# A new order of steps beside the weight conversions, and own orders for the first two periods, in a fused attention and squared-ReLU kernel

## The chip, the cores and the metric

The kernel runs on one core of one Trainium2 chip. The metric is the device time of one launch in microseconds (us), the median of several runs. The profile is one execution of the program, with every instruction of the engines: PE (matmuls; PEld is its weight load), DVE (vector), ACT (scalar, activations), POOL (GpSimd) and SP, which only issues DMAs.

## The reference

Thresholded attention over 8 batches of 8 heads, 576 positions, head size 64; its output, 4608 tokens of 512, goes through a two-layer network.

```python
def _attn_ref(q, k, v, tau):
    scale = 1.0 / np.sqrt(q.shape[-1])
    scores = scale * np.matmul(q, k.transpose(0, 1, 3, 2))
    thresh = np.max(scores, axis=-1, keepdims=True) - tau
    scores = np.where(scores >= thresh, scores, -1000000000.0)
    scores = scores - np.max(scores, axis=-1, keepdims=True)
    attn = np.exp(scores)
    attn = attn / (np.sum(attn, axis=-1, keepdims=True) + 1e-09)
    return np.matmul(attn, v)

def _moe_ref(x, w_in, w_out):          # x: (4608, 512), w_in: (512, 2048), w_out: (2048, 512)
    h = np.maximum(x @ w_in, 0.0)
    return h * h @ w_out
```

The inputs q, k and v are float32; the two weight matrices come as float64, so each weight is two 32-bit words, a low and a high one.

## The kernel before

The kernel has three stages: attention, from the start to about 512 us; the hidden layer (L825); and the output layer (L960). The two layers use a scheme with fewer block products and many block sums; the change touches only the attention.

Attention works on pairs of heads (32 pairs) in units. A unit is 128 query rows of one pair, and after the four units of each of two pairs comes one unit that holds the last 64 rows of both: 144 units. A *period* p handles the pair of units A = 2p and B = 2p + 1. `period(p)` runs a list of named steps, each of which issues instructions; an engine executes its own instructions in the order in which the list names them, and waits only on semaphores. So the list sets the order on each engine, and a step far down one engine's queue may hold up another engine. There is one period from p = -2 to p = 74; scores start at p = 0, and the values' matmuls of a pair of units follow two periods later.

The steps of a period, with the engine and the line in the profile:

- SA, SB (PE, L434): scores of the units A and B into the banks of the PSUM tile `sc`. SA also writes the last 64 keys of both units, into banks 1 and 4; SB writes banks 2 and 3, SA's main part banks 0 and 5.
- topA0, topA1, topB0, topB1 (DVE, L452): copy a head's 576 scores from PSUM to SBUF, with the (negated) maximum accumulated.
- leastA, leastB (POOL, L459, 128x2): the threshold of both heads of a unit, from the two tops.
- powA0 ... powB1 (ACT, L462): the exponential.
- maskA0 ... maskB1 (DVE, L467): compare the scores with the threshold and multiply by the exponential, with the sum accumulated; both inputs are in SBUF. The masks need the power and the least.
- over (POOL, L474) and inv (DVE, L477): the sum plus 1e-9 and its reciprocal, for the previous period's units.
- U, V, W (PE, L380 and L515): transposes of the weights in three parts, U and V into the two banks of the pool `pt`, which has one buffer, W into banks 2 and 3 of `sc`; eU, eV, eW (ACT, L523) evict them.
- T (PE, L398) transposes queries or keys of a coming pair; eT (ACT, L403 and L411) evicts them, scaled where they are queries, and asks for the next loads of queries or keys on SP's queue. T's places are `spots()`, parts of the banks 1 and 4 of `sc`.
- PV (PE, L532): the values' matmuls into banks 0 and 5; x (ACT in a converting period, DVE in others) copies them out, xm (POOL, L654) multiplies them by the reciprocal, issues the next load of values and the writes of x.
- fetch, c1 to c6: conversion of one weight chunk (128 x 512 float64) to float32. fetch loads the chunk of period p + 2; c1 (ACT, L205) takes the absolute value of the high words; c2 (POOL, L212) scales the low words by 2^-29; c3 (POOL, L219) clamps the high words; one period later c4 (DVE, L227, shift and mask), c5 (DVE, L235, merges the sign, two inputs in SBUF) and c6 (POOL, L245, adds the low words).

Chunks are begun in the periods 2 to 33, so the periods 2 to 34 are *converting* ones and use the list CONVERTING; the others use PLAIN. The touch function orders instructions that share a PSUM bank: an instruction waits for the last one of each other engine that touched the same bank.

The beginning is written out: loads of the first pair, 15 warm-up transposes of PE (`keep_busy`), the turns of the first pair, then the periods; after period 0 come 20 more warm-up transposes (L1012).

Of the kernel before, what the change touches and what calls it, by code (L numbers as in the profile page):

```python
# [10 lines left out]
FP32 = mybir.dt.float32  # L11
# [37 lines left out]
def kernel(  # L49
# [27 lines left out]
    P = 128  # L77
# [7 lines left out]
    BANK = 512  # L85
# [305 lines left out]
    def turn(i, which, spots, other=None):  # L391

        nat, to = loaded.pop((i, which)), places(i)
        of = [nat[:, t, :] for t in range(FULL)] + ([loaded.pop((i, 2))] if which else [])
        for t, x in enumerate(of):
            for r, (spot, at) in enumerate(spots):
                rows = ds(r * HALF, HALF)
                made = nc.tensor.transpose(spot[:, ts(t, HALF)], x[rows, :], ident[rows, rows])  # L398
                touch("turns", made, at, BANK)
        half = FULL * HALF  # L400

        def scaled(to, spot):
            touch("turned", nc.scalar.activation(out=to, in_=spot[0], func=AF.Identity, scale=qscale[:, :]), spot[1], BANK, i)  # L403

        def then():
            part = lambda r, x, n: (spots[r][0][:, ds(x, n)], spots[r][1])
            if which:
                for r, n in ((0, half), (1, half + REST)):
                    spot = part(r, 0, n)
                    copy_by = other if r and other else nc.scalar.copy  # L410
                    touch("turned", copy_by(to[1][:, ds(r * half, n)], spot[0]), spot[1], BANK, i)  # L411
                scaled(to[2], part(0, half, REST))
                ask_ahead(i, 1)
            else:
                for r in range(2):
                    scaled(to[0][:, ds(r * half, half)], part(r, 0, half))
                ask_ahead(i, 0)

        return then
# [68 lines left out]
    for g in range(2, 2 * len(pairs)):  # L488
        two, x = divmod(g - 4, 4)
# [93 lines left out]
    def converts(p):  # L583
        return is_wide and (has_chunk(p) or has_chunk(p - 1))

    def has_chunk(p):
        return p in starts

    def begun(n):
        return starts.get(n)  # L590

    PLAIN = """
# [2 lines left out]
        maskB1  # L595
    """.split()
    CONVERTING = """
        fetch SA U eU T SB topA0 s1 c1 topA1 topB0 c3 V PV leastA over powA0 topB1
        powA1 powB0 c4 eT inv x maskA1 maskA0 W leastB maskB0 c5 eV c2 powB1 c6 eW maskB1 xm
    """.split()  # L600

    def spots():
        return [(sc[:, ds(b * BANK + REST, (FULL + 1) * HALF)], b * BANK) for b in (1, 4)]
# [4 lines left out]
    def period(p):  # L608

        A, B_, a, b = 2 * p, 2 * p + 1, 2 * p - 2, 2 * p - 1  # L610
        m, turns = p - 2, TURNS.get(p, ())
        late, pt = {"W": []}, {}

        def fills(f, m):
            if has(2 * m):
                pt[f] = pt_pool.tile([P, 2, BANK], FP32, tag="pt", name="pt")
                fill(m, f, pt[f])

        def evict(f, m):
            if has(2 * m):  # L620
                filled(m, f, pt[f], 2 * BANK if f == "W" else None)

        def W():
            if has(2 * m + 2):
                pt["W"] = middle()
                fill(m + 1, "W", pt["W"], 2 * BANK)

        def turn_some():
            late["turn"] = [turn(g // 2, g % 2, spots()) for g in turns]

        def PV():
            if has(2 * m):
                values(m)

        def values_out():
            if not has(2 * m):
                return
            late["x"] = x = sb.tile([P, 2, P], FP32, tag="x", bufs=2, name="x")
            for j in range(2):
                from_ = sc[:, ds(5 * j * BANK, P)]  # L640
                if converts(p):
                    made = nc.scalar.copy(x[:, j, :], from_)
                else:
                    made = nc.vector.tensor_tensor(  # L644
                        out=x[:, j, :], in0=from_, in1=wT[m][:, ts(SCALE_AT + j, P)], op=ALU.mult
                    )
                touch("x", made, 5 * j * BANK, P, m)

        def given_out():
            if has(2 * m):  # L650
                x = late.pop("x")
                if converts(p):
                    both = x[:, :, :].rearrange("p j n -> p (j n)")
                    nc.gpsimd.tensor_tensor(out=both, in0=both, in1=wT[m][:, ds(SCALE_AT * P, 2 * P)], op=ALU.mult)  # L654
                wT.pop(m)
                valued(m)
                give_x(m, x)
            ask(False)

        def scored_a():  # L660
            if has(A):
                scores(A, False)
                scores(A, True)
                scores(B_, True)
                softmax(A)

        def scored_b():
            if has(A):
                scores(B_, False)
                softmax(B_)  # L670

        def every(key):
            for then in late.get(key, ()):
                then()

        steps = {
            "U": lambda: fills("U", m), "V": lambda: fills("V", m + 1), "W": W, "T": turn_some,
            "eU": lambda: evict("U", m), "eV": lambda: evict("V", m + 1), "eW": lambda: evict("W", m + 1),
            "eT": lambda: every("turn"),
            "SA": scored_a, "SB": scored_b,  # L680
            "PV": PV, "x": values_out, "xm": given_out,
            "c1": lambda: convert1(begun(p)), "c2": lambda: convert2(begun(p)),
            "c3": lambda: convert3(begun(p)), "c4": lambda: convert4(begun(p - 1)),
            "c5": lambda: convert5(begun(p - 1)), "c6": lambda: convert6(begun(p - 1)),
            "s1": lambda: sums_due(p) and sums_step(), "s2": lambda: sums_due(p) and p < 60 and sums_step(), "fetch": lambda: fetch(begun(p + 2)),
        }
        steps["over"] = lambda: do(a, "over")
        steps["inv"] = lambda: do(a, "inverse")
        for letter, n in (("A", A), ("B", B_)):
            for what, name in (("least", "least"),):  # L690
                steps[what + letter] = lambda n=n, name=name: do(n, name)
            for what, name in (("top", "top"), ("pow", "power"), ("mask", "mask")):
                for j in range(2):
                    steps[f"{what}{letter}{j}"] = lambda n=n, name=name, j=j: do(n, name, j)
        for name in CONVERTING if converts(p) else PLAIN:
            steps[name]()
        for n in (A, B_):
            if has(n) and units[n][1] == FULL:
                for i in units[n][0]:
                    turned.pop(i)  # L700
# [301 lines left out]
    with tc.manual_schedule():  # L1002
        with ExitStack() as stack:
            sc = stack.enter_context(tc.tile_pool(name="sc", bufs=1, space=PSUM)).tile([P, 6 * BANK], FP32, name="sc")
            pt_pool = stack.enter_context(tc.tile_pool(name="pt", bufs=1, space=PSUM))

            def keep_busy(times, to=None):

                if to is None:
                    to = pt_pool.tile([P, 2, BANK], FP32, tag="pt", name="idle")[:, 0, 0:P]  # L1010
                for _ in range(times):
                    nc.tensor.transpose(to, ident[:, :], ident[:, :])  # L1012

            load_q(0)
            load_k(0)
            read_tau()
            first = sb.tile([P, 4, 4], FP32, tag="small", bufs=4, name="small")
            nc.scalar.activation(out=first[:, 0, :], in_=ident[:, 0:4], func=AF.Exp)
            load_v(0)
            keep_busy(15)  # L1020
            pq = pt_pool.tile([P, 2, BANK], FP32, tag="pt", name="pq")
            turn(0, 0, [(pq[:, r, :], None) for r in range(2)])()
            keep_busy(8, sc[:, ds(5 * BANK, P)])
            turn(0, 1, spots(), nc.vector.tensor_copy)()
            for i in range(1, 3):
                load_v(i)
            for p in range(-2, NU // 2 + 3):
                period(p)
                if p == 0:
                    keep_busy(20)  # L1030
                if X_FIRST <= p < X_FIRST + 4:
                    load_x(0, XPARTS[p - X_FIRST :][:1])
                if p == X_FIRST + 4:
                    summing.append(prepare_x(0, lambda op, out, x, y: op(nc.gpsimd, out, x, y)))
            for _ in range(60):
                sums_step()
            ask()
# [186 lines left out]
```

## Time and profile before

| what | value |
|---|---|
| median of 3 runs | 1308.91 us (1307.8 to 1309.66) |
| the profiled execution | 1308.12 us, span 1306.3 us |
| busy over the span | PE 98%, DVE 77%, ACT 65%, POOL 70% |
| masks (L467) | x288, 237.4 us, 860 ns mean |
| tops (L452) | x288, 205.0 us, 747 ns mean |
| low-word scaling c2 (L212) | x32, 65.1 us, 2035 ns mean |
| clamp c3 (L219) | x32, 19.6 us, 613 ns mean |
| c6 (L245) | x32, 1.48 us each |
| least (L459) | x144, 65.3 us, 453 ns mean |
| warm-up after period 0 | x20, 2.40 us from 11.41 us |

A line of the timeline has the start in us, the duration in us, engine, line of the kernel, operation, output and inputs with their sizes, and in brackets the idle time of that engine ahead of it with what ended it. On DVE a row's duration runs on a little into the next row, so lengths are best taken from start to start. The means of a group mix rows beside other work with rows alone.

### The profile page before, as it was taken

What the parts mean: (1) busy time and instruction counts of PE and PEld (TensorE: products, weight loads), DVE (VectorE), ACT (ScalarE), POOL (GpSimd) and SP (SyncE); (2) the same over time, 40 slices, a digit from 0 to 9 for tenths busy, and PEclk for the clock granted to TensorE, in tenths of its full rate; (3) what the DMA queues carried; (4) which work ended last, traced back from release to release, by engine and by line L of the source; (5) the groups of instructions that cost most, each with busy time, mean ns of one, the idle gap of its engine ahead of it and who ended that gap; (6) DMA issues with size and microseconds to landing.
All of it is one profiled execution on the core that took longest, in us unless ns stands there. A gap on an engine that the chain in (4) does not pass through costs nothing.

```text
span 1306.3 us, 47872 instructions
## 1 busy us (share of the span) xinstructions
PE 1284.5 (98%) x19483; PEld 1159.8 (89%) x19483; DVE 1010.8 (77%) x2431; ACT 845.7 (65%) x1498; POOL 916.4 (70%) x1023
## 2 busy tenths in 40 slices
PE   8999999999999999999999999999999999999998
PEld 5777777677777777999999999999999999999998
DVE  5999999999999996877787778777646654665463
ACT  5999999888898985657665766675523432433240
POOL 2777778755555320978897789768777777777775
PEclk9999999999999999999999999999999999999999
DMA  6565666544333313466556665569645234522511
GB/s 153 145 160 140 169 182 188 147 103 104 89 78 79 79 41 80 133 200 218 182 181 194 203 208 164 180 247 393 245 158 162 63 105 158 162 68 96 162 34 33
DMA packets 247035, 192.12 MB, mean 147 GB/s; under 512 B 97184, under 2 KB 195488, under 8 KB 246816
## 3 DMA queue, kind: packets, MB, share of 16 engines
q1 hardware_dynamic: 245504, 188.66, 48.5%
q8 instruction: 153, 2.51, 0.8%
q14 instruction: 66, 0.54, 0.2%
q10 hardware_dynamic: 1312, 0.41, 0.1%
HBM read 116.65 MB, written 72.35 MB: 145 GB/s over the span
## 4 chain that ended last, share of the span: by engine, by line
PE 87%; ACT 5%; DMA 3%; DVE 3%; issue 1%; POOL 1%; SPq 0%; ACTq 0%; DVEq 0%; POOLq 0%
PE po L960 29%; PE ph L825 28%; PE sc L532 11%; PE sc L434 10%; PE pt L380 5%; DVE arena L452 3%; ACT arena L462 2%; PE sc L515 2%; DMA wall<-w 2%; PE sc L398 2%; ACT arena L523 1%; PE sc L380 1%; DMA g<-arena 1%; ACT arena L403 0%; ACT c L771 0%
## 5 line engine op out<-in xcount | busy, mean ns | idle before, releaser
L125 POOL TENSOR_TENSOR arena<-arena 128x512 f32<-128x512 f32 (+1 forms) x314 | 378.1, 1223 | 129.1 <-DVE arena L125 115.1
L960 PE MATMUL po<-wall,arena 128*128 128x128 f32 x3528 | 394.7, 275 | 1.4 <-ACT arena L737 1.4
L960 PEld LDWEIGHTS po<-wall,arena 128*128 128x128 f32 x3528 | 394.3, 192 | 1.8 <-ACT arena L737 1.8
L825 PE MATMUL ph<-arena,wall 128*128 128x128 f32 x3528 | 394.2, 275 | 0.7 <-DVE arena L644 0.7
L825 PEld LDWEIGHTS ph<-arena,wall 128*128 128x128 f32 x3528 | 394.0, 192 | 0.8 <-issue 0.8
L125 DVE TENSOR_TENSOR arena<-ph,arena 128x512 f32<-128x512 f32 x378 | 256.3, 688 | 86.3 <-PE ph L825 63.2
L122 POOL TENSOR_TENSOR arena<-arena 128x128 f32<-128x128 f32 (+2 forms) x314 | 255.4, 814 | 53.8 <-DMA arena<-w 37.6
L125 DVE TENSOR_TENSOR arena<-po,arena 128x128 f32<-128x128 f32 x378 | 108.4, 290 | 168.6 <-PE po L960 164.5
L467 DVE SCALAR_TENSOR_TENSOR arena<-arena 128x576 f32<-128x576 f32 x288 | 237.4, 860 | 1.3 <-POOL arena L459 0.8
L452 DVE TENSOR_SCALAR_CACHE_REDUCE arena<-sc 128x576 f32<-128x576 f32 x288 | 205.0, 747 | 14.6 <-ACT arena L523 4.8
L462 ACT ACTIVATE arena<-arena 128x576 f32<-128x576 f32 x288 | 208.1, 773 | 11.8 <-DVE arena L452 8.5
L771 ACT COPY c<-arena 128x512 f32<-128x512 f32 (+1 forms) x303 | 173.5, 579 | 49.6 <-DVE arena L122 41.7
L532 PEld LDWEIGHTS sc<-arena 64*64 64x64 f32 x5760 | 159.2, 133 | 36.7 <-DVE arena L452 20.2
L532 PE MATMUL sc<-arena 64*64 64x128 f32 (+1 forms) x5760 | 180.8, 262 | 2.7 <-DVE arena L452 1.3
L434 PE MATMUL sc<-arena 64*64 64x64 f32 (+1 forms) x2304 | 176.9, 414 | 6.2 <-ACT arena L403 4.2
L122 DVE TENSOR_TENSOR arena<-arena,c 128x512 f32<-128x512 f32 (+1 forms) x267 | 174.9, 663 | 5.5 <-ACT c L771 4.0
L523 ACT COPY arena<-pt 128x1024 f32<-128x1024 f32 x144 | 146.4, 1017 | 30.5 <-PE pt L380 29.4
L737 ACT COPY arena<-po 128x128 f32<-128x128 f32 x63 | 16.6, 264 | 186.7 <-PE po L960 184.0
L380 PEld LDWEIGHTS pt<-ident,arena 64*128 64x128 f32 x2304 | 83.4, 139 | 39.4 <-ACT arena L523 30.1
L737 ACT COPY arena<-ph 128x512 f32<-128x512 f32 x63 | 36.6, 581 | 123.1 <-PE ph L825 122.5
L434 PEld LDWEIGHTS sc<-arena 64*64 64x64 f32 x2304 | 74.3, 134 | 45.1 <-ACT arena L403 15.1
L380 PE MATMUL pt<-ident,arena 64*128 64x64 f32 x2304 | 102.2, 228 | 2.3 <-ACT arena L523 2.3
(50 smaller groups left out, 922.2 us busy)
## 6 DMA issues: line engine op xcount, KB each, us to landing
g<-arena SPq DMA_DIRECT2D x144, 256.0 KB, 2.6
arena<-g SPq DMA_DIRECT2D x144, 256.0 KB, 4.6
w<-arena SPq DMA_DIRECT2D x60, 256.0 KB, 2.4
wall<-w SPq DMA_DIRECT2D x49, 256.0 KB, 5.2
arena<-w SPq DMA_DIRECT2D x44, 256.0 KB, 3.3
arena<-in_v_dram SPq DMA_DIRECT2D x32, 288.0 KB, 4.0
out_dram<-arena SPq DMA_DIRECT2D x70, 128.0 KB, 2.2
arena<-in_q_dram SPq DMA_DIRECT2D x64, 128.0 KB, 4.0
```

The costliest lines, as they stand in the source:

```text
L122: e.tensor_tensor(out=out, in0=x, in1=y, op=ALU.subtract)
L125: e.tensor_tensor(out=out, in0=x, in1=y, op=ALU.add)
L380: made = nc.tensor.transpose(pt[:, r, ts(slot, HALF)], of[rows, :], ident[rows, rows])
L434: made = nc.tensor.matmul(sc[at, ds(to, count)], lhs, kT[rows, ds(at_k, count)], start=True, stop=True)
L452: made = nc.vector.tensor_scalar(out=s[:, j, :], in0=sc[:, ds(at, S)], scalar1=1.0, scalar2=None, op0=ALU.mult, op1=ALU.min, accum_out=nmx ...
L462: nc.scalar.activation(out=w[:, :, j, :], in_=of(j), func=AF.Exp, bias=nmx[:, j : j + 1], scale=-1.0)
L467: nc.vector.scalar_tensor_tensor(out=w[:, :, j, :], in0=of(j), scalar=thr[:, j : j + 1], in1=w[:, :, j, :], op0=ALU.is_le, op1=ALU.mult, a ...
L523: touch("weights", nc.scalar.copy(joined(to), whole(pt, 0, count)), at, 2 * BANK, m)
L532: made = nc.tensor.matmul(sc[ds(u * D, D), ds(5 * j * BANK + row, count)], loaded_v[i][rows, (c - (u != j)) % CH, :], wT[m][rows, ds(weigh ...
L771: nc.scalar.copy(c, y)
L825: nc.tensor.matmul(to[:, j, :], W_IN[m, k][:, ts(j, P)], of[k][:, m - 1, :], start=(not more and j == 0), stop=True, skip_group_check=True,)
L960: nc.tensor.matmul(to, g[:, j, :], w[:, j, :], start=(not more and j == 0), stop=(j == 3), skip_group_check=True)
```

## The change

Three things change. The list of the converting periods is replaced by another one. The periods 0 and 1 get lists of their own, `BEGIN_WITH`, in place of PLAIN. In periods below 2 the turned queries and keys go to a tile of the pool `pt`, instead of the spots in the banks 1 and 4 of `sc`, where scores are written too. Around the first turn, the loads of the second pair's queries and keys are asked for ahead of the first values' load, and the 20 warm-up transposes after period 0 are left out. No computation is added or removed.

```diff
     CONVERTING = """
-        fetch SA U eU T SB topA0 s1 c1 topA1 topB0 c3 V PV leastA over powA0 topB1
-        powA1 powB0 c4 eT inv x maskA1 maskA0 W leastB maskB0 c5 eV c2 powB1 c6 eW maskB1 xm
+        s1 fetch SA T U c1 topA1 topA0 leastA eU SB over topB0 PV c2 powA1 powA0 maskA1
+        powB0 topB1 c4 eT inv x V powB1 leastB maskA0 maskB0 c3 c5 eV W maskB1 c6 xm eW
     """.split()
+
+    BEGIN_WITH = {
+        0: """
+            SA SB fetch topA0 T topA1 leastA topB0 topB1 leastB powA0 powA1 eT powB0 powB1
+            maskA0 maskA1 maskB0 maskB1
+        """.split(),
+        1: """
+            SA SB T eT fetch over topA0 topA1 leastA inv V topB0 topB1 leastB powA0 powA1 eV W
+            powB0 eW maskA0 maskA1 powB1 maskB0 maskB1
+        """.split(),
+    }
...
         def turn_some():
-            late["turn"] = [turn(g // 2, g % 2, spots()) for g in turns]
+            free = None
+            if turns and p < 2:
+                pq = pt_pool.tile([P, 2, BANK], FP32, tag="pt", name="pq")
+                free = [(pq[:, r, :], None) for r in range(2)]
+            late["turn"] = [turn(g // 2, g % 2, free or spots()) for g in turns]
...
-        for name in CONVERTING if converts(p) else PLAIN:
+        for name in BEGIN_WITH.get(p) or (CONVERTING if converts(p) else PLAIN):
             steps[name]()
...
             nc.scalar.activation(out=first[:, 0, :], in_=ident[:, 0:4], func=AF.Exp)
+            ask_ahead(0, 0)
+            ask_ahead(0, 1)
             load_v(0)
...
             for p in range(-2, NU // 2 + 3):
                 period(p)
-                if p == 0:
-                    keep_busy(20)
```

The order list of PLAIN, which the periods 0 and 1 used, is `SA c3 T topA0 over U eU s1 SB topA1 powA1 leastA topB0 powB0 c1 s2 PV c4 V fetch inv powA0 c5 topB1 powB1 eT maskA1 x xm W eV maskA0 leastB c2 c6 eW maskB0 maskB1`.

## The prediction

> **What bounds the kernel now.** I read the windows first, to see which engine is full in the stretch that the change touches.
>
> ```profile
> 160.00:180.00 20.00, 19.70 (x464) 14.47 (x462) 20.00 (x55) 19.06 (x34) 16.94 (x21) 1.00 0.66 178
> 300.00:320.00 20.00, 19.75 (x546) 14.88 (x540) 19.54 (x60) 17.77 (x28) 11.42 (x15) 1.00 0.49 118
> ```
>
> Columns: PE, PEld, DVE, ACT and POOL busy, clock, DMA share, GB/s. In the converting stretch (first row) DVE is busy 20.00 of 20 us; in the plain one PE is the fullest. So in the 33 converting periods every nanosecond of DVE counts. The period is the distance between two reciprocals (L477): 163.48 to 170.56, 7.08 us; nearly all of them are 7.05 to 7.10, 7.07 in the middle.
>
> Next, the timeline of DVE over one such period, and of POOL beside it.
>
> ```profile
> 163.57 0.78 DVE L467 SCALAR_TENSOR_TENSOR arena<-arena 128x576 f32<-128x576 f32 x1
> ...
> 164.28 1.22 DVE L467 SCALAR_TENSOR_TENSOR arena<-arena 128x576 f32<-128x576 f32 x1
> ...
> 165.43 0.81 DVE L467 SCALAR_TENSOR_TENSOR arena<-arena 128x576 f32<-128x576 f32 x1
> ...
> 166.17 0.68 DVE L235 SCALAR_TENSOR_TENSOR arena<-arena 128x512 int32<-128x512 int32 x1
> 166.78 0.81 DVE L467 SCALAR_TENSOR_TENSOR arena<-arena 128x576 f32<-128x576 f32 x1
> ...
> 167.51 0.75 DVE L452 TENSOR_SCALAR_CACHE_REDUCE arena<-sc 128x576 f32<-128x576 f32 x1
> ```
>
> ```profile
> 163.34 0.38 POOL L459 TENSOR_SCALAR arena<-arena,tau_p 128x2 f32<-128x2 f32 x1
> 163.79 2.04 POOL L212 TENSOR_SCALAR arena<-arena 128x512 int32<-128x512 uint32 x1
> 167.00 1.48 POOL L245 TENSOR_TENSOR arena<-arena 128x512 int32<-128x512 int32 x1 [1.17 <-DVE arena L235]
> 168.44 0.72 POOL L654 TENSOR_TENSOR arena<-arena 128x256 f32<-128x256 f32 x1
> 169.14 0.62 POOL L219 TENSOR_SCALAR arena<-arena 128x512 f32<-128x512 f32 x1
> 169.74 0.30 POOL L459 TENSOR_SCALAR arena<-arena,tau_p 128x2 f32<-128x2 f32 x1
> 170.09 0.23 POOL L474 TENSOR_SCALAR arena<-arena 128x4 f32<-128x4 f32 x1
> ```
>
> From start to start the masks (L467) take 0.71, 1.15, 0.74 and 0.73. The second is long by 0.41 in every converting period: POOL's low-word scaling c2 (L212) began 0.22 into the first mask, so its reading falls to the moment when the second should start. The third mask is not longer, though c2 runs 0.40 into it. The tops (L452, which read PSUM) take 0.68 each beside c6 (L245), xm (L654) and c3 (L219): no cost. So a POOL operation costs DVE time beside an operation that reads two SBUF tiles, and none beside a top. Without the 0.41, DVE's period would be 7.08 - 0.41 = 6.67. ACT's own operations, start to start from 161.37 to 168.30, are about 6.83 (three powers 1.99, turn 0.83, x 0.32, fourth power 0.67, evictions 0.91 + 0.63 + 0.91, c1 0.60): the next floor.
>
> Two more places show how the engines meet. A 128x2 least (L459) that starts inside a mask, and c4 (L227) that starts inside c3:
>
> ```profile
> 13.29 0.81 DVE L467 SCALAR_TENSOR_TENSOR arena<-arena 128x576 f32<-128x576 f32 x1
> 13.47 0.80 POOL L459 TENSOR_SCALAR arena<-arena,tau_p 128x2 f32<-128x2 f32 x1 [1.05 <-DVE arena L452]
> ...
> 233.57 0.61 POOL L219 TENSOR_SCALAR arena<-arena 128x512 f32<-128x512 f32 x1 [0.73 <-ACT arena L205]
> ...
> 233.90 0.56 DVE L227 TENSOR_SCALAR arena<-arena 128x512 int32<-128x512 int32 x1
> ```
>
> The least takes 0.80 instead of 0.30: it ends 0.24 after the mask (14.03). c4 takes 0.56 instead of 0.42: POOL was there first.
>
> **The new converting period.** Nothing is added; the lists decide. DVE's order becomes topA1, topA0, topB0, maskA1, topB1, c4, inverse, maskA0, maskB0, c5, maskB1. POOL's becomes leastA, over, c2, leastB, c3, c6, xm. Put down with the durations above, from the start of topA1:
>
> - DVE without waits: topA0 0.68, topB0 1.36, maskA1 2.03, topB1 2.77, c4 3.45, inverse 3.79, maskA0 3.88, maskB0 4.59, c5 5.33, maskB1 5.94, end 6.67.
> - POOL: c6 starts 0.22 into the last mask, as now, and goes 0.93 past its end (1.44 to xm); xm 0.70 to 1.63; leastA 0.35 to 1.98 (its other input, topA0, is there at 1.5); over 0.33 to 2.31; c2 from 2.31 to 4.34.
>
> c2 thus starts 0.28 into maskA1, nearly as now, but its reading (done 0.88 after its start: 0.49 to the second mask and its 0.41 of delay) falls beside topB1, which costs nothing. So the 0.41 is gone. Three things take its place.
>
> First, leastB stands behind c2 on POOL. It is dispatched at 4.34, inside maskA0 (3.88 to 4.59), and by the 13.47 row ends 0.24 after that mask: 4.83. maskB0 needs it and is next on DVE; with 0.07 for the hand-over (POOL's gap between operations) it starts at 4.90 instead of 4.59: 0.31. Queued behind it are c5 and maskB1, and the next period's tops. Bounds: 0, if c2 is over by 3.6, to 0.31.
>
> Second, c3 moves from beside the tops, where it was free, to behind leastB, at 4.9. From there to 6.67 DVE runs only operations with two SBUF inputs, so c3 reads at one of their borders. It is a one-input 128x512 read as c2 is: 0.41. Bounds: 0, if it slips into a gap, to 0.47 (how far into c3 the c4 at 233.90 waited). I take 0.41.
>
> Third, c4 at 3.45 now lies inside c2 (2.31 to 4.34). No row shows that pair. Lower bound 0: the third mask runs beside c2's second half unharmed. Upper bound: c4 beside c3 waited until 0.14 before c3's end, so 4.34 - 0.14 - 3.45 = 0.75. I take 0, since the nearest rows with c2 itself are the masks.
>
> [...]
>
> Sum: 6.67 + 0.31 + 0.41 = 7.39, above ACT's 6.83, so DVE stays the bound. Against 7.07 that is +0.32; c2 and c3 run in 32 periods: +10.2 us. Other engines: values (2.2 to 2.4 us) start at 1.5, after topA0, so x on ACT is at about 3.9, and the next eU ends near 7.9, 0.5 into the next period, before powA1's input (0.7). SB waits for eW, about 6.4, and ends before topB0 needs it at 8.7. PE's own work, about 6.5, fits.
>
> **The start.** This is the gain. Now DVE waits at three places: topA0 at 10.57, since the turn ahead of it waits for the second pair's queries (10.00); 16.63, since scores wait for a turn in banks 1 and 4; and above all 25.37:
>
> ```profile
> 16.63 0.76 DVE L452 TENSOR_SCALAR_CACHE_REDUCE arena<-sc 128x576 f32<-128x576 f32 x1
> ...
> 25.37 0.76 DVE L452 TENSOR_SCALAR_CACHE_REDUCE arena<-sc 128x576 f32<-128x576 f32 x1 [2.80 <-issue]
> ```
>
> In the new order scores A and B run at 7.64 to 10.0 without the turn between them; topA0 at 9.1; four tops to 11.8; four masks (the second 0.15 late behind leastB) to 14.9. ACT turns the queries at 11.2 between powers. Period 1: scores need only tops (11.8), done 13.5; key turn 14.0, evicted 14.9, V to 15.6; tops 14.9 to 17.7 (inverse included); ACT powers to 17.05, eV 17.95, powB0 18.6, eW 19.2, powB1 19.9; masks end at 20.8. Scores of period 2 run from 18.4, the turn is done at 20.2, so the tops of period 2 start at 20.8 instead of 25.37: -4.5 us. The 20 warm-up matmuls (2.40 us at 11.41) were in a gap; without them PE's clock may be lower for a while (it was 0.91 in 20 to 40 us already), which I price at 0 to 1.8 us of PE time (0.09 x 20), with PE waiting anyway. The nine query and key issues of the second pair now go ahead of the first values on SP's queue; the values are first used at 27.0. The second weight chunk goes behind two pairs of keys, from 16.43 to about 20, landing 5 us later, before its c1 near 28. So -4.5, bounds -2.5 to -5.
>
> **Sum.** The profiled execution has span 1306.3 and 1308.12 us in all, 0.8 below the median 1308.91. +10.2 - 4.5 = +5.7: 1313.8 on that execution, 1314.6 on the median.
>
> **Rivals.**
>
> *c4 locked out.* c4 waits for c2: +0.75. leastB then finishes before maskA0 ends, so its 0.31 falls away; c3's 0.41 stays: 6.67 + 0.75 + 0.41 = 7.83, +0.76 x 32 = +24.3, less 4.5: 1328.7. For it: c4 at 233.90. Against: the third mask.
>
> *c2 is short when no mask follows it (the other side).* c2's 2.04 was always taken beside three masks. If its second half was itself held up and it ends by 3.6 here, leastB is done before maskA0 and its wait is gone. It decides at c2's end: before 3.9 no wait, after it 0.31. Then 6.67 + 0.41 = 7.08, level with now, and the start remains: 1304.4. Against: c2's length is 2.00 to 2.07 whatever stands behind the second mask. [...]
>
> *Neither least nor c3 costs anything.* Then ACT's 6.83 binds, 6.85 with a hand-over: -0.22 x 32 - 4.5 = -11.5, 1297.4. For it: only gaps in DVE that c3 would have to meet.
>
> **Chances.** Forecast 0.42, c4 locked out 0.24, short c2 0.20, neither 0.10, and 0.04 for waits not seen that make it slower. About 0.2%, 2.6 us, is what a measurement can tell from no change. Faster: 0.10 + 0.20 for the two cases below, 0.01 for a cheaper forecast case: 0.31. Same: 0.07, from the forecast case with half of its price. Slower: 0.62. The range goes from 1301 (short c2 with the start's upper bound and a cheaper c3) to 1330 (c4 locked out) and leaves out "neither" and the tails. The two slower cases alone would be 1311 to 1330.
>
> **What would show it.** The reciprocals 7.39 apart; no long mask at c2's start, an idle DVE of about 0.3 ahead of maskB0, released by POOL L459; a mask or c5 of about 1.15 beside c3; topA1 of period 2 near 20.8. Wrong: c4 of 1.1 us (first rival), L212 well under 2 us (second), or a converting period under 7.

## The result, and the profile after

The changed kernel takes 1313.62 us, the median of 13 runs (1310.93 to 1314.60); the kernel before took 1308.39 us beside it (13 runs, 1306.38 to 1309.76). The ratio is 1.0039, with an interval of 1.0032 to 1.0046: slower by 5.2 us. The profiled execution of the changed kernel takes 1311.95 us, with a span of 1310.2 us.

The windows of the changed kernel, over the same two stretches as before (columns PE, PEld, DVE, ACT and POOL busy, clock, DMA share, GB/s):

```profile
160.00:180.00 20.00, 17.14 (x434) 11.95 (x430) 19.61 (x52) 19.16 (x33) 15.23 (x20) 1.00 0.65 174
300.00:320.00 20.00, 19.76 (x540) 14.83 (x539) 19.47 (x60) 17.78 (x28) 11.66 (x16) 1.00 0.46 113
```

In the converting stretch DVE now has gaps: 19.61 of 20 us, where it had 20.00. PE's busy time went from 19.70 to 17.14, but it was not the bound here and it is not now. The plain stretch is as it was. The distance of two reciprocals in the converting periods is 7.28 or 7.29 us (158.91 to 166.19, for one), where it was 7.07.

One converting period on DVE, from its timeline. It begins with the topA1 at 155.12; topA0 and topB0 are not shown:

```profile
157.16 0.80 DVE L467 SCALAR_TENSOR_TENSOR arena<-arena 128x576 f32<-128x576 f32 x1
...
157.90 0.74 DVE L452 TENSOR_SCALAR_CACHE_REDUCE arena<-sc 128x576 f32<-128x576 f32 x1
...
158.57 0.41 DVE L227 TENSOR_SCALAR arena<-arena 128x512 int32<-128x512 int32 x1
158.91 0.16 DVE L477 RECIPROCAL arena<-arena 128x4 f32<-128x4 f32 x1
159.00 0.78 DVE L467 SCALAR_TENSOR_TENSOR arena<-arena 128x576 f32<-128x576 f32 x1
...
159.98 1.15 DVE L467 SCALAR_TENSOR_TENSOR arena<-arena 128x576 f32<-128x576 f32 x1 [0.19 <-POOL arena L459]
...
161.06 0.68 DVE L235 SCALAR_TENSOR_TENSOR arena<-arena 128x512 int32<-128x512 int32 x1
161.67 0.81 DVE L467 SCALAR_TENSOR_TENSOR arena<-arena 128x576 f32<-128x576 f32 x1
```

POOL's timeline beside it:

```profile
157.44 2.08 POOL L212 TENSOR_SCALAR arena<-arena 128x512 int32<-128x512 uint32 x1
159.62 0.33 POOL L459 TENSOR_SCALAR arena<-arena,tau_p 128x2 f32<-128x2 f32 x1
159.91 0.61 POOL L219 TENSOR_SCALAR arena<-arena 128x512 f32<-128x512 f32 x1
161.89 1.48 POOL L245 TENSOR_TENSOR arena<-arena 128x512 int32<-128x512 int32 x1 [1.37 <-DVE arena L235]
```

From start to start: maskA1 0.74, topB1 0.67, c4 0.34. All three run with c2 (157.44 to 159.52) beside them, and none is longer than alone. maskA0 ends at 159.71 (0.71). Then DVE stands until 159.98, 0.27 us (the row's 0.19 is what is left behind the 0.07 of the accumulator's read), for leastB, which came out of the queue behind c2 at 159.62, inside maskA0, and ended at 159.95. maskB0 takes 1.08 instead of 0.74, with c3 (159.91 to 160.52) across its start: 0.34. So 7.28 = 6.67 + 0.27 + 0.34.

At the start, three rows of DVE's timeline show period 2 beginning to wait again; beside them, from PE's, the scores A of period 2:

```profile
22.41 0.76 DVE L452 TENSOR_SCALAR_CACHE_REDUCE arena<-sc 128x576 f32<-128x576 f32 x1 [0.60 <-PE sc L398]
...
24.73 0.76 DVE L452 TENSOR_SCALAR_CACHE_REDUCE arena<-sc 128x576 f32<-128x576 f32 x1 [0.87 <-PE sc L434]
...
33.57 0.82 DVE L467 SCALAR_TENSOR_TENSOR arena<-arena 128x576 f32<-128x576 f32 x1 [1.27 <-ACT arena L462]
```

```profile
19.39 2.36 PE L434 MATMUL sc<-arena 64*64 64x512 f32 x24
```

topA1 of period 2 starts at 22.41 (25.37 before, 20.8 forecast). Of that lead almost nothing is left one period later: the reciprocals of the periods 1, 2 and 3 stand at 16.95, 26.82 and 35.33, against 18.67, 28.09 and 35.64 before. From period 3 to 33 the changed kernel takes 218.54 us and the kernel before 213.48: +5.06. Thirty periods at 0.215 would be 6.45; most of the difference is two longer periods of the kernel before (7.65 and 7.77). Behind the conversions 0.5 comes back (the three periods to the reciprocal at 274.08 take 20.21 instead of 20.73).

### The profile page after: what moved, and what is told of

It is laid out like the page before. It is cut to its first block, busy times and chain, and to the rows that moved or that the text cites. A ratio compares the mean times of both kernels' runs of the same rounds, so it can differ in the third digit from the quotient of the medians.

```text
span 1310.2 us, 47769 instructions
## 1 busy us (share of the span) xinstructions
PE 1265.7 (97%) x19463; PEld 1140.1 (87%) x19463; DVE 1010.9 (77%) x2431; ACT 845.5 (65%) x1498; POOL 915.6 (70%) x1023
## 4 chain that ended last, share of the span: by engine, by line
PE 78%; ACT 4%; DVE 3%; DMA 1%; issue 1%; POOL 1%; ACTq 0%; DVEq 0%; POOLq 0%
PE ph L840 30%; PE po L975 27%; PE sc L532 7%; PE sc L434 6%; PE pt L380 4%; DVE arena L452 2%; PE sc L398 1%; ACT arena L523 1%; ACT arena L462 1%; PE sc L515 1%; DMA wall<-w 1%; DMA arena<-g 0%; DVE arena L125 0%; PE sc L380 0%; DVE arena L122 0%
## 5 line engine op out<-in xcount | busy, mean ns | idle before, releaser
L532 PEld LDWEIGHTS sc<-arena 64*64 64x64 f32 x5760 | 153.9, 133 | 82.3 <-DVE arena L452 68.7
L532 PE MATMUL sc<-arena 64*64 64x128 f32 (+1 forms) x5760 | 169.9, 262 | 27.1 <-DVE arena L452 26.9
L434 PE MATMUL sc<-arena 64*64 64x64 f32 (+1 forms) x2304 | 172.7, 414 | 3.5 <-ACT arena L403 2.3
L434 PEld LDWEIGHTS sc<-arena 64*64 64x64 f32 x2304 | 63.3, 134 | 48.6 <-issue 26.3
L459 POOL TENSOR_SCALAR arena<-arena,tau_p 128x2 f32<-128x2 f32 x144 | 62.8, 436 | 52.0 <-DVE arena L452 47.0
```

Source lines behind the costliest of these rows:

```text
L434: made = nc.tensor.matmul(sc[at, ds(to, count)], lhs, kT[rows, ds(at_k, count)], start=True, stop=True)
L532: made = nc.tensor.matmul(sc[ds(u * D, D), ds(5 * j * BANK + row, count)], loaded_v[i][rows, (c - (u != j)) % CH, :], wT[m][rows, ds(weigh ...
```

## The experiments

Each kernel was timed beside the kernel before on one chip; ratios are to that kernel, and since the chips differ, versions are compared by them. A period is the distance of two reciprocals. Each version has one profile. Edits are to the changed kernel. The first five share out the loss in the list, the others look for the gain at the start.

**The old list with the new beginning.**

```diff
     CONVERTING = """
-        s1 fetch SA T U c1 topA1 topA0 leastA eU SB over topB0 PV c2 powA1 powA0 maskA1
-        powB0 topB1 c4 eT inv x V powB1 leastB maskA0 maskB0 c3 c5 eV W maskB1 c6 xm eW
+        fetch SA U eU T SB topA0 s1 c1 topA1 topB0 c3 V PV leastA over powA0 topB1
+        powA1 powB0 c4 eT inv x maskA1 maskA0 W leastB maskB0 c5 eV c2 powB1 c6 eW maskB1 xm
     """.split()
```

> The new beginning with the old list for the converting periods. My theory: the loss sits in the steady converting period (7.285 against 7.07 us, 32 times, some 6.9 us) and the beginning is a small gain, so this kernel has the old period of 7.07 and ends 0 to 2 us below the kernel before. Rival: the beginning is where the time went (PE's half clock, the second weight chunk late) and the list is harmless; then this kernel is 4 to 6 us above the kernel before.

Measured: 1307.8 against 1309.12, ratio 0.9993 (0.9981 to 1.0004). The period is 7.07; the reciprocals of the periods 2 and 3 stand at 26.21 and 33.70, the latter 1.94 earlier than in the kernel before.

**The new list with the old beginning.**

```diff
-            if turns and p < 2:
+            if False:
...
-        for name in BEGIN_WITH.get(p) or (CONVERTING if converts(p) else PLAIN):
+        for name in CONVERTING if converts(p) else PLAIN:
...
-            ask_ahead(0, 0)
-            ask_ahead(0, 1)
...
                 period(p)
+                if p == 0:
+                    keep_busy(20)
```

> The old beginning with the new list for the converting periods. My theory: period 7.28 from the first converting periods on, 5 to 7 us above the kernel before (32 x 0.21 = 6.9, less about 1.3 for two long periods of the kernel before at 127 and 227 us that the new list may not have). Rival (the beginning costs): within 1 us of the kernel before.

Measured: 1312.76, ratio 1.0031 (1.0019 to 1.0043), the period 7.28. So the loss is in the list, 4.1 us by the ratio and 2.5 to 5.6 by its interval, somewhat less than the 5 to 7 expected; the new beginning by itself brings 0.9 us, and by its interval between 2.5 us and a loss of 0.5.

**Without c3.**

```diff
-... maskA0 maskB0 c3 c5 eV W ...
+... maskA0 maskB0 c5 eV W ...
```

> The changed kernel without c3: the clamp of the high words is left out. My theory: c3 reads at the border of two masks, which makes maskB0 1.08 instead of 0.74 us; without it maskB0 is 0.74, the period 7.28 - 0.34 = 6.94, and the time 32 x 0.34 = 11 us below the changed kernel, about 1302. Rival: the long maskB0 comes from leastB, which ends just before it, or from the tail of c2; then maskB0 stays near 1.08 and the period at 7.28.

Measured: 1306.55, ratio 0.9983 (0.9974 to 0.9993); the period is 6.95. DVE's timeline:

```profile
161.34 0.78 DVE L467 SCALAR_TENSOR_TENSOR arena<-arena 128x576 f32<-128x576 f32 x1
...
162.32 0.82 DVE L467 SCALAR_TENSOR_TENSOR arena<-arena 128x576 f32<-128x576 f32 x1 [0.19 <-POOL arena L459]
...
163.06 0.69 DVE L235 SCALAR_TENSOR_TENSOR arena<-arena 128x512 int32<-128x512 int32 x1
```

maskB0 is back at 0.74 (162.32 to 163.06), and the wait for leastB ahead of it stays (162.05 to 162.32). So in an undisturbed period c3 costs the 0.34 and nothing else: 7.285 - 0.34 = 6.945. On the time the expectation missed: 1306.55, not 1302. From the reciprocal of period 3 to that of period 33 the run takes 210.76 us, 7.78 less than the changed kernel and not 30 x 0.34 = 10.2; four periods of 7.20 to 8.06 take the rest.

The same profile shows something of the start, since up to the tops of period 2 this kernel is the changed one. topA1 of period 2 starts at 20.61, as early as forecast. Then c1 waits for the second weight chunk, and the reciprocal of period 3 stands at 35.56:

```profile
31.47 0.66 ACT L205 ACTIVATE arena<-arena 128x512 f32<-128x512 f32 x1 [3.37 <-DMA arena<-in_moe_w_in_dram]
```

**c2 on a quarter of its words.** Two kernels: in the first c6 adds that quarter to all four (`wide` reads it four times, `four` views a tile as four quarters; their definitions are left out here), in the second it subtracts the high words from themselves.

```diff
             lo = parts[m][0]
+            lo = lo[:, 0:128]
             nc.gpsimd.tensor_scalar(out=lo, in0=lo.bitcast(U32), scalar1=2.0**-29, ...)
...
-        nc.gpsimd.tensor_tensor(out=a, in0=hi, in1=lo, op=ALU.add)
+        nc.gpsimd.tensor_tensor(out=four(a), in0=four(hi), in1=wide, op=ALU.add)      # first kernel
+        nc.gpsimd.tensor_tensor(out=a, in0=hi, in1=hi, op=ALU.subtract)               # second kernel
```

> The changed kernel with c2 on 128 of the 512 low words (c6 adds these four times, so the other words get a wrong low part). My theory: leastB waits for c2's end and then for maskA0, which leaves DVE idle 0.27 us ahead of maskB0; with c2 over in under 1 us leastB runs before maskA0, the idle time goes and c3 still costs 0.34 at a border: period 7.01, 32 x 0.27 = 8.6 us below the changed kernel, about 1305. Rival: the wait has another cause (powB0 or leastB's own input), and the period stays at 7.28.

Measured: 1315.33, ratio 1.0044 (1.0028 to 1.0061), the period 7.325. That missed, by a side effect. The wait ahead of maskB0 is gone, but the c6 with the repeated operand takes 1.82 instead of 1.48 us, leastA comes out later behind it, and maskA1 now waits 0.27 for that. So its period says nothing on what leastB costs. At the start, where it too is the changed kernel, topA1 of period 2 starts at 21.16, and c1 then waits 5.82 us for the second chunk, to 33.69; the reciprocal of period 3 stands at 37.79. The second kernel:

> As e4_short_c2, but with c6 in its own shape (it subtracts the high words from themselves, so the weights are zero), since the c6 of e4_short_c2 took 1.82 instead of 1.48 us and held leastA back. My theory: no idle time ahead of maskB0, none ahead of maskA1 either, c3 still 0.34 to 0.37: period 7.01 to 7.04, 8 us below the changed kernel. Rival: leastB stays late because it meets maskA0 whenever it comes; then the period stays at 7.28.

Measured: 1307.98 against 1307.95, ratio 0.9999 (0.9989 to 1.0009), the period 7.01 to 7.02. DVE's timeline, and POOL's (an added line moves the line numbers: L468 is the mask, L236 c5, L460 the least, L220 c3):

```profile
162.31 0.78 DVE L468 SCALAR_TENSOR_TENSOR arena<-arena 128x576 f32<-128x576 f32 x1
...
163.03 1.15 DVE L468 SCALAR_TENSOR_TENSOR arena<-arena 128x576 f32<-128x576 f32 x1
...
164.11 0.68 DVE L236 SCALAR_TENSOR_TENSOR arena<-arena 128x512 int32<-128x512 int32 x1
```

```profile
162.06 0.40 POOL L460 TENSOR_SCALAR arena<-arena,tau_p 128x2 f32<-128x2 f32 x1 [0.36 <-DVE arena L453]
162.44 1.13 POOL L220 TENSOR_SCALAR arena<-arena 128x512 f32<-128x512 f32 x1
```

The masks stand back to back, and maskB0 still takes 1.08. c3 begins inside maskA0, 0.13 after its start, takes 1.13 instead of 0.61, and lies across the border of the two masks. leastB's place behind c2 is thus worth 7.285 - 7.015 = 0.27, c3's place 0.34, each shown by itself. The time is some 5 us below the changed kernel by the ratios, not the 8 expected; some periods are longer here, up to 8.28.

**Neither of the two.** The short c2, and no c3.

> The changed kernel with the short c2 and without c3, weights zero. My theory: both prices go, DVE would need 6.67, and ACT's own 6.83 is the floor: period 6.83 to 6.87. Rival: another wait of DVE (leastA ahead of maskA1, powA1) holds it at 6.94 or more.

Measured: 1301.03, ratio 0.9947 (0.9929 to 0.9965). Most periods are near 6.67 or near 6.84, close to the prediction's sums for DVE (6.67) and for ACT (6.83); some are longer, up to 8.98. As the shorter ones lie below 6.83, ACT's sum is not the floor of every period, and the expected 6.83 to 6.87 was met only in part. Which engine sets which period is not shown.

**The second chunk's fetch ahead of the keys' loads.** In the changed kernel these rows belong together, one from SP's timeline, one from ACT's:

```profile
26.93 1.32 SPq L191 DMA_DIRECT2D arena<-in_moe_w_in_dram  x2
```

```profile
31.21 0.68 ACT L205 ACTIVATE arena<-arena 128x512 f32<-128x512 f32 x1 [1.40 <-DMA arena<-in_moe_w_in_dram]
```

The load was asked for at 26.93, not at the 20 of the prediction: fetch is named behind eT, which asks for the keys of two pairs and their last queries, and those fourteen issues stand ahead of it on SP, from 15.96 on. c1 waits 1.40 for it, the powers queue behind c1 on ACT, and maskA1 (33.57) waits 1.27 for them.

```diff
         1: """
-            SA SB T eT fetch over topA0 topA1 leastA inv V topB0 topB1 leastB powA0 powA1 eV W
+            SA SB T fetch eT over topA0 topA1 leastA inv V topB0 topB1 leastB powA0 powA1 eV W
```

> The changed kernel with the second weight chunk's load ahead of the keys' loads in period 1, as it was before. My theory: in the changed kernel c1 of period 3 waited 1.40 us for that chunk and DVE 1.27 us behind it; now the reciprocal of period 3 comes about 1.2 us earlier (34.1 instead of 35.3) and the total 1.2 us lower. Rival: the keys then come late for the turn of period 3 and nothing is gained.

Measured: 1310.3, ratio 1.0012 (1.0003 to 1.0021). The load is asked for at 16.77, c1 starts at 29.46 without a wait, and the reciprocal of period 3 stands at 33.78 instead of 35.33: 1.55 of the missing lead, of which 0.20 was there at the reciprocal of period 2 already. The expectation (1.2) held there. By the ratios this version is some 3.5 us below the changed kernel; its profile shows 1.55 at the end of the conversions, and what makes the rest is open.

**Filling PE where it stands idle, to keep its clock.** PE's scores A of period 2 take 2.36 us in the changed kernel, at a granted clock of one half. Windows laid along the half clock, of the changed kernel and then of the kernel before:

```profile
13.87:17.28 3.41, 1.47 (x30) 1.04 (x26) 3.41 (x12) 2.17 (x6) 0.38 (x2) 1.00 1.03 326
17.28:20.69 3.41, 2.55 (x28) 1.44 (x32) 3.39 (x10) 3.15 (x5) 0.94 (x2) 0.50 0.74 144
20.69:24.11 3.42, 3.42 (x52) 2.16 (x48) 2.27 (x6) 1.66 (x3) 0.16 (x1) 0.50 0.35 80
24.11:27.50 3.39, 3.39 (x108) 2.87 (x104) 2.77 (x8) 3.11 (x8) 2.51 (x4) 1.00 0.28 61
```

```profile
18.70:22.15 3.45, 1.41 (x24) 0.87 (x28) 3.42 (x12) 3.45 (x8) 0.80 (x1) 1.00 0.81 209
22.15:25.56 3.41, 3.41 (x52) 2.40 (x48) 0.61 (x3) 1.62 (x3) 0.00 (x0) 0.50 0.41 92
25.56:29.00 3.44, 3.44 (x96) 2.53 (x88) 3.44 (x12) 3.44 (x7) 1.85 (x4) 1.00 0.30 66
```

The half clock lasts 6.83 us in the one, 3.41 in the other. The new beginning does not always bring 6.83, though. Of the runs that are the changed kernel up to period 2, the one without c3 has 3.41 us of half clock (19.10 to 22.51), and the first one with the short c2 has none, with nothing added to PE. From the reciprocal of period 1 to that of period 2 these two take 8.89 and 8.52 us, and the changed kernel and the two others with 6.83 us of half clock 9.87 to 9.93: a price of about 1.35 us for the 6.83. The first attempt to shorten it:

```diff
             late["turn"] = [turn(g // 2, g % 2, free or spots()) for g in turns]
+            if turns and p == 1:
+                keep_busy(8, pq[:, 1, 384:512])
...
             steps[name]()
+            if p == 1 and name == "V":
+                keep_busy(6, sc[:, 0:P])
```

> The changed kernel with 14 warm-up transposes back in PE's gaps of period 1 (8 behind the turn, 6 behind V). My theory: PE's half clock from 17.4 to 24.2 us, which makes scores A of period 2 take 2.36 instead of 1.27 us, comes from PE's idle time ahead of it; with it filled the clock stays at 1.00 in most of 16 to 24 us, the turn of period 2 is done about 1.5 us earlier and the reciprocal of period 2 comes at about 25.5 instead of 26.8. Rival: the clock goes down for another reason (the loads' traffic or the start itself), and the same windows show 0.66 and 0.50.

Measured: 1313.55, ratio 1.0040 (1.0025 to 1.0055). The half clock still lasts 6.83 us, and the reciprocal of period 2 is at 27.75, later than the 26.82 of the changed kernel. The eight transposes go into the bank that the turn's eviction reads; that the eviction waits for them is the author's reading, given without a figure. This expectation fell. The next one puts back the 20 warm-ups of the kernel before, beside the early fetch:

```diff
                 period(p)
+                if p == 0:
+                    keep_busy(20)
```

> The changed kernel with the early chunk load and the 20 warm-up transposes after period 0 back in their old place. One theory: those 20 held the clock up, so half clock lasts 3.4 us as in the kernel before instead of 6.8, and the reciprocal of period 2 comes about 1 us earlier than 26.62. Rival: half clock belongs to the new beginning's gaps in period 1 and stays 6.8 us; the 20 then only delay scores A of period 1, and the reciprocals of periods 1 and 2 come 1 to 2 us later.

Measured: 1314.52, ratio 1.0042 (1.0029 to 1.0056). PE's timeline:

```profile
12.94 3.71 PE L1027 MATMUL idle<-ident 128*128 128x128 f32 x20 [1.91 <-ACT arena L403]
```

The half clock falls to 3.41 us, as hoped, but now on the 20 themselves: they stand in a bank of `pt`, wait 1.91 us for ACT's eviction of the turn out of it, and then take 3.71 us ahead of period 1. Its reciprocal comes at 19.61, that of period 2 at 28.80 (26.62 without them).

**The old list, the new beginning and the early fetch.** The two edits of the first and the sixth experiment together.

> The new beginning with the old list for the converting periods and the second weight chunk's load ahead of the keys' loads. My theory: the beginning's gain stays (the reciprocal of period 3 at about 33.4 instead of 35.64 in the kernel before), the period is 7.07 again, and it ends 2 to 3 us below the kernel before, so faster than both kernels. Rival: the beginning's gain is given back later, in the waits for the converted chunks' writes, and it is level with the kernel before.

Measured: 1304.27 against 1308.79, ratio 0.9964 (0.9950 to 0.9977). It beats both kernels. The reciprocal of period 3 stands at 33.53, and the period is 7.07. How much of this the fetch brings is open: without it (the first experiment, ratio 0.9993) the reciprocal of period 3 is only 0.17 later, at 33.70, and c1 waited 0.40 for the chunk; and the profiled execution here, 1306.88, is the slowest of the five. With the 20 warm-ups as well:

> e8_list_fetch with the 20 warm-up transposes back. Where the 20 hold the clock up, 1 us below e8_list_fetch; where they only delay, 1 to 2 us above it.

Measured: 1307.51, ratio 0.9995 (0.9982 to 1.0008), the reciprocal of period 3 at 34.62, 1.09 later than without the 20 (33.53). They take 4.07 us there, from 12.59, and cost more than they bring.

**Twelve transposes in PE's own gap.** To the version with 1304.27:

```diff
             steps[name]()
+            if p == 1 and name == "V":
+                keep_busy(12, sc[:, 0:P])
```

> The version with the old list, the new beginning and the earlier fetch (1304.27), with 12 more transposes of PE in period 1 behind V, where PE stood idle from 16.35 to 17.80 us for the tops; they write bank 0 of the scores, which the tops have left. Theory: the half clock follows on a stretch of 3.41 us in which PE was busy less than about half. Ahead of it PE was busy 1.47 of 3.41 us in the changed kernel, 1.41 in the kernel before, 1.51 in the version with the earlier fetch and the old list, 1.73 with the two groups of transposes, 1.50 with the 20 warm-ups; no stretch at full clock with 2.37 or more was followed by it. With 6 or 7 of the 12 in the stretch that ends near 17.2 us PE is busy about 2.4 of it, so the half clock should not come there: scores A of period 2 take about 1.3 instead of 2.36 us, the reciprocal of period 3 stands at about 32.3 instead of 33.53, and the kernel is about 1 us faster, 1303. Rival, the share of PE's busy time does not decide, or these transposes do not count: the half clock lasts 6.83 us as in the last version, the reciprocal of period 3 is at 33.5 to 33.9, and the time 1304.3 to 1304.7.

Measured: 1306.11 against 1308.32, ratio 0.9986 (0.9977 to 0.9995). Windows and, below, PE's timeline:

```profile
16.00:20.00 4.00, 2.48 (x36) 2.04 (x40) 2.47 (x10) 2.68 (x4) 0.93 (x2) 1.00 1.05 274
20.00:24.00 4.00, 4.00 (x89) 2.43 (x85) 4.00 (x12) 3.44 (x6) 0.64 (x2) 1.00 0.75 202
```

```profile
16.25 1.53 PE L1029 MATMUL sc<-ident 128*128 128x128 f32 x12 [0.52 <-DVE arena L452]
...
19.86 1.27 PE L434 MATMUL sc<-arena 64*64 64x512 f32 x24
```

On the clock the expectation held: it is 1.00 in every 4 us slice from 8 to 28 us, the scores A of period 2 take 1.27 instead of 2.36, and the reciprocal of period 3 is at 32.35. That the twelve did this is likely, but not shown: the first run with the short c2 has no half clock either, without them. What speaks for them is that with them PE was busy for at least 1.80 us in any stretch of 3.41 us from 8 to 25 us, wherever it is laid, and in that run for only 0.98 in some. On the time the expectation missed: the ratio is no better than the 0.9964 without the twelve. Two things are seen. topB0 of period 1 waits 1.53 for the transposes and starts at 17.82 (17.01 without them), so that from the reciprocal of period 1 to that of period 3 this run is only 0.37 shorter (16.23 against 16.60); the rest of its lead, 0.81, was there at the reciprocal of period 1 already, ahead of the added work. And the lead of 1.18 is gone at period 33 (246.91 against 246.90), in three longer periods of 8.13, 7.81 and 7.68 where the other profile had one of 8.13 and one of 7.23. In the last two of the three, c1 waits for the writing out of an earlier chunk (1.40 and 0.91, DMA w<-arena); ACT's timeline of the second:

```profile
166.35 0.68 ACT L205 ACTIVATE arena<-arena 128x512 f32<-128x512 f32 x1 [1.40 <-DMA w<-arena]
```

Whether an earlier start brings these waits on, or whether they fall where they will, one profile of each doesn't settle.

## Why the prediction was right, and by how much it was off

It said 1314.6 and slower; 1313.6 was measured. The sign was right, and so were the mechanisms in the list; the gain at the start was not. That the total came within about 1 us is luck: the list's loss was put at 10.2 and the start's gain at 4.5, and the profiles show about 4.5 (5.06 less the 0.5 that comes back) and 0.3. Two errors of opposite sign covered for each other, in a wide range (1301 to 1330).

- **The stretch of the second mask goes.** Right. c2 started 2.32 us into the period (2.31 forecast), 0.28 into maskA1, and the 0.88 us that it was given for its reading ended beside topB1 (at 158.32; topB1 from 157.90, 0.67 long). No mask is long at c2's start (maskA1 0.74). The 0.88 us, an estimate, fits the kernel before (0.86 to 0.92 in all but the first converting period), though the two terms named beside it, 0.49 and 0.41, add up to 0.90.
- **leastB behind c2.** Right. c2 ended at 4.40 (4.34), leastB at 4.83 (4.83), maskB0 began at 4.86 (4.90). The term of 0.31 measured 0.27, and the short c2 took away just that.
- **c3 at a border of masks.** Right in kind, 0.34 instead of 0.41, shown by leaving c3 out. The 0.41 was borrowed from c2, as the nearest row; c3 is a shorter operation (0.61 against 2.08). Whether that is why it costs less, no run shows.
- **c4 inside c2 at no cost.** Right: 0.34 from start to start, and 0.33 in the run where no c2 lies beside it (neither of the two). The rival that c4 is locked out is refuted: c4 ran wholly inside c2, between 158.57 and 158.91, and maskA0, with two SBUF inputs, took its usual 0.71 from 159.00 on, while c2 went on to 159.52. What c3 and c2 did cost a mask is the 0.34 and the 0.41, each less than the POOL operation itself (0.61 and 2.04). Both stand in the length of the mask, without a wait in its brackets (163.03 in the second run with the short c2, 164.28 in the kernel before), so it is too narrow to say that an engine waits only on semaphores.
- **The rival of the short c2** is refuted in this place: c2 took 2.08, and the point from which it decides, 3.9, was passed by half a microsecond. Its premise was half right: c2 is shorter, 1.65 and 1.64, where it does not begin inside a mask (in the changed kernel at 24.64, with a top right behind it, and at 32.41, with DVE idle). By these rows it is the mask it begins in that makes it long, not the masks behind it, and the new list lets it begin inside maskA1.
- **The rival that neither costs anything** is refuted by the 0.27 and the 0.34. The ACT floor of 6.83 that it rests on is not exact either: its listed terms add up to 6.86, and the run with neither has periods of 6.67.
- **The sum of a period.** 7.39 forecast, 7.285 measured, so +0.215 instead of +0.32, or +6.9 instead of +10.2 over 32 periods.
- **The start.** This is the step that failed: -4.5 forecast, with bounds of -2.5 to -5, and -0.31 measured at the reciprocal of period 3 (the whole new beginning, with the old list behind it, brought -1.94). Three parts of it were off.
  - The second chunk's load was put at about 20 us and at no cost. It was issued at 26.93, and the sixth experiment got 1.35 back in that one period by asking earlier. The rows for it were there: in the kernel before the same fourteen issues take SP from 19.11 to 28.73, 9.6 us, where the prediction allowed 3.6. This part alone can take the whole gain: in the run without c3 and in the first with the short c2 the tops of period 2 began at 20.61 and 21.16, near the forecast, and c1 then waited 3.37 and 5.82 for the load, so that period 3 was no earlier than in the changed kernel.
  - The half clock of PE was priced at 0 to 1.8 us and put in at 0, "with PE waiting anyway". But the scores of period 2 were not waiting work: they took 2.36 instead of 1.27, DVE's tops waited 0.60 and 0.87 for PE, and 6.83 us of half clock cost about 1.35 in this period, by the estimate above. Whether the removed warm-ups are the reason is not shown, since the same beginning also came out with 3.41 us of half clock and with none; put back, they cost more than they brought.
  - The masks of period 1 ended a microsecond later than worked out (21.8 instead of 20.8), from topA0 on, which started at 9.92 instead of 9.1. That differs between executions: in the run without c3 topA0 started at 9.19. There the eight transposes of PE ahead of the first keys' turn took 1.09 us, and 1.82 in the changed kernel's profile.

The profile's own sum is -0.3 at the reciprocal of period 3, +5.1 from there to period 33 and -0.5 behind it, about +4.2 us to the end of the conversions, and the span is 3.9 longer.

## What to carry to other kernels

When an engine is full, the order on its neighbour's queue is part of its bound: an operation of 0.3 us that is named behind one of 2 us comes late by what is left of the long one. Here leastB (0.33) stood behind c2 (2.08), came out inside a mask and cost DVE 0.27 us a period; the old list names it ahead of the long one, and DVE does not wait for it there. The new list with only that exchanged was not run. Where the profile shows operations of one engine made longer beside another's, as masks were here by c2 and c3 and the tops, which read PSUM, were not (0.67 beside c2), lay the long ones beside operations that keep their length, and follow in the new order what each of them meets then; here one collision of 0.41 was exchanged for one of 0.34 and a wait of 0.27. A lead that is won at the start lasts only until the first load that lands too late for it (c1 waited 1.40, 3.37 and 5.82 for the second chunk in three profiles here): follow each issue through its queue to the first step that uses it, and count the issues that stand ahead of it. And one profile is one execution: here the same beginning came out with three different lengths of half clock.

## What the runs showed of the hardware that was not expected

- c2 (128x512, uint32 to int32 on POOL) made the mask that starts early in it longer, and nothing later: in the kernel before the second mask takes 1.15, the 0.41 too much being over 0.86 to 0.92 us after c2's start if it is put at the mask's start (an estimate), and in the remaining 1.2 us of c2 masks and c4 ran at their usual length (0.74 from 165.43 on there, 0.34 and 0.71 from 158.57 and 159.00 on in the changed kernel). In these rows c2 begins inside a mask; it takes 2.00 to 2.23 us then, in the two kernels. Begun outside a mask it takes 1.55 to 1.65 (two in the changed kernel, four in the run without c3). The difference is about the 0.46 us that are left of the mask in which it begins (157.44 to 157.90).
- A 128x2 operation of POOL that began inside a mask ended 0.24 after it: 159.95 after 159.71, and 14.27 after 14.03 at the start of the kernel before.
- The half clock of PE came in whole pieces of 3.41 us (3.41 or 6.83 long) in the twelve profiles that have one, each time behind 3.41 us at full clock in which PE was busy for 1.3 to 1.85 us: 1.47 and 1.41 in the windows above, 1.85 in the run without c3. In that run a stretch with 2.27 was not followed by it; whether a bound lies between the two, no run shows. A piece at half clock with 2.55 us of work was followed by another, one with 2.95 (the new list with the old beginning) was not. The same beginning had 6.83, 3.41 or none, and in the changed kernel no gap of PE in or across the stretch ahead of the half clock was longer than 1.45 us. What sets where the pieces begin is not shown.
